# Queries of clusters without keys evened out by the mask alone, operand tiles by halves, and new engine orders, in a two-layer attention kernel

## The chip, the core and the metric

One NeuronCore of a Trainium2 chip runs the program. Its engines work side by side: TensorE (PE) multiplies matrices, PEld is its queue of weight loads, VectorE (DVE), ScalarE (ACT) and GpSimd (POOL) work elementwise, SyncE (SP) issues the DMA transfers. The metric is the device time of one run in microseconds. The kernel before took 713.66 us, the median of three runs (713.56 to 715.48).

## What is computed

The first layer is attention within clusters (4 batches, 8 heads, 768 positions, 64 wide, 16 clusters); its output is the input of a mixture of 4 attention experts, of which each position uses 2.

```python
def _attn_ref(q, k, v, centroids):
    ...
    q_assign = np.argmax(np.einsum('bhsd,hcd->bhsc', q_n, c_n), axis=-1)
    k_assign = np.argmax(np.einsum('bhsd,hcd->bhsc', k_n, c_n), axis=-1)
    mask = q_assign[:, :, :, None] == k_assign[:, :, None, :]
    scores = scale * np.matmul(q, k.transpose(0, 1, 3, 2))
    scores = np.where(mask, scores, -1000000000.0)
    ...  # softmax over keys, then attn @ v

def _moe_ref(x, w_gate, wq, wk, wv, wo):
    ...  # the two largest of x @ w_gate give the weights w
    for e in range(E):
        ...  # causal softmax attention with q, k, v = x @ wq[e], x @ wk[e], x @ wv[e]
        ye = a @ v @ wo[e]
        ...  # out += w * ye where e is one of the two
```

A query whose cluster holds no key has the same score, -1e9, for all keys: its attention is even over all 768 positions.

## The kernel before

The work is 24 steps: 16 *pairs* (two heads of one batch) and 8 expert pairs. Each has an operand part (`attention_operands`, `moe_operands`) and a core (`core`), and three sets of operand tiles `tk`, `tq` rotate, so that operands are made while earlier cores run. All products are in fp32r; a factor is split into a high part (rounded) and a low part (the rest), and high x high, high x low and low x high are added.

*Operands of a pair.* k and q are loaded and transposed (L626), copied from PSUM, and split; the low part is a subtraction on VectorE that reads PSUM (L639 for k, L782 for q). Scores with the centroids (L650), transposed (L662), give one-hot rows of the cluster by five VectorE steps (L668 to L676). Then keys are counted: six matmuls with ones (L685) and four VectorE steps that multiply the one-hot of q by min(count, 1) (L695), which clears the rows of queries without keys. The one-hot is transposed (L703), ScalarE makes `rows` (L706: 0 or 1 for q, 0 or -2^33 for k), and one matmul per head (L766) spreads over 64 rows whether a query has keys: the gate, with which VectorE multiplies q (L776; for the first half of pair 0 also L770, straight into `tq`). Only then q is split. SP moves the parts and the one-hot rows into `tk` and `tq`.

*Core of a pair.* Row scores (L1088: contraction over 64 high rows and 16 one-hot rows) give, by a maximum on VectorE (L1098, joined in L1104), the largest score of each query. The six columns of maxima are transposed (L1110; for pair 0 L1113), negated (L1126 or ScalarE) and moved into a row of `tq`. Scores (two matmuls, L1165 over 128 rows and L1166 over 97) then come out with mask and maximum in them, ScalarE takes exp (L1171), and p is weighted with v in a tile 64 columns wide (av, L1209). GpSimd and VectorE add up p (L478, L479), and matmuls of a tile 32 wide sum it over keys (L1233).

*Order.* Every engine's order is a written list of operation numbers, `ORDER`. A planner with prices for operations decides only how the five lists interleave and which buffer each tile takes. While it sees TensorE wait, and until the `av` buffer is first taken, it puts filler matmuls into TensorE's list (L1337: 256 columns of ones).

Of the kernel before, what the change touches and what calls it, by code (L numbers as in the profile page):

```python
# [244 lines left out]
class Plan:  # L245
# [1146 lines left out]
```

## Time and profile before

| | |
|---|---|
| median of 3 runs | 713.66 us (713.56 to 715.48) |
| profiled execution, span | 713.4 us |
| TensorE busy | 696.5 us (98%), 4562 matmuls |
| VectorE busy | 568.3 us (80%) |
| ScalarE busy | 363.0 us (51%) |
| GpSimd busy | 295.1 us (41%) |
| chain that ended last | 80% TensorE, 6% VectorE, 5% DMA |

The pairs run first, the expert pairs behind them. A matmul that the profile gives 0.34 us can start 0.17 us after the one before: successive matmuls overlap, so the spacing of the starts is what one costs.

### The profile page before, as it was taken

To read this page: it belongs to the slowest core of one execution; us is meant where nothing else is said; L and a number is where in the kernel's file an instruction comes from. 1 tells how busy PE (TensorE), PEld (TensorE's weight loads), DVE (VectorE), ACT (ScalarE), POOL (GpSimd) and SP (SyncE) were. 2 spreads that over 40 slices of the span, in tenths; PEclk is the share of its full clock that TensorE was granted. 3 is DMA by queue.
4 is the path that set the end of the run, shared out by engine and by line. 5 is a ranking of instruction groups with operands and counts; after the bars stand their busy time and mean duration, and the time that the engine had idled before them with its cause. 6 is when DMAs were issued, how large, how long until landed. Compare 5 with 4: busy or idle time off the path is not lost.

```text
span 713.4 us, 13574 instructions
## 1 busy us (share of the span) xinstructions
PE 696.5 (98%) x4562; PEld 521.5 (73%) x4562; DVE 568.3 (80%) x1293; ACT 363.0 (51%) x899; POOL 295.1 (41%) x236
## 2 busy tenths in 40 slices
PE   6999999999999999999999999999999999999997
PEld 4666768667677676676676678868977987987776
DVE  6979899878989888888888876895688688577843
ACT  4365657456466466456465633364345435333542
POOL 5033456564555574856778422241111203210410
PEclk9999999999999999999999999999999999999999
DMA  6695765677677576667586564455355555445223
GB/s 194 167 218 124 186 161 133 146 198 198 182 206 187 142 198 150 174 166 190 156 195 177 135 182 135 111 143 133 106 145 142 141 142 157 104 101 162 77 82 120
DMA packets 79793, 109.97 MB, mean 154 GB/s; under 512 B 23936, under 2 KB 63212, under 8 KB 79724
## 3 DMA queue, kind: packets, MB, share of 16 engines
q1 hardware_dynamic: 79724, 109.11, 58.3%
q8 instruction: 36, 0.59, 0.4%
q14 instruction: 33, 0.27, 0.1%
HBM read 36.54 MB, written 12.91 MB: 69 GB/s over the span
## 4 chain that ended last, share of the span: by engine, by line
PE 80%; DVE 6%; DMA 5%; SPq 4%; ACT 3%; issue 1%; ACTq 0%; DVEq 0%
PE av L1209 19%; PE st L1165 11%; PE row L1088 11%; PE st L1166 10%; PE misc L870 9%; PE misc L922 5%; SPq L466 4%; PE misc L1322 4%; PE misc L1233 3%; PE misc L626 2%; DMA tq<-hi 2%; DVE mx L1098 2%; DMA kt<-in_k_dram 2%; PE misc L650 1%; DMA vm<-x 1%
## 5 line engine op out<-in xcount | busy, mean ns | idle before, releaser
L1098 DVE TENSOR_REDUCE mx<-row 128x1 f32<-128x384 f32 (+1 forms) x442 | 232.6, 548 | 41.8 <-PE row L1088 37.8
L1165 PE MATMUL st<-tq,tk 128*128 128x384 f32 (+2 forms) x528 | 182.6, 348 | 3.2 <-ACT p L1171 2.1
L1171 ACT ACTIVATE p<-st 128x384 f32<-128x384 f32 (+2 forms) x304 | 130.0, 458 | 109.6 <-PE st L1166 68.2
L1166 PE MATMUL st<-tq,tk 97*128 97x384 f32 (+2 forms) x528 | 173.7, 332 | 0.0
L1088 PE MATMUL row<-tk,tq 80*128 80x384 f32 (+4 forms) x506 | 168.0, 359 | 1.7 <-DMA tq<-hi 1.2
L1165 PEld LDWEIGHTS st<-tq,tk 128*128 128x128 f32 x528 | 99.9, 189 | 21.4 <-issue 7.0
L1088 PEld LDWEIGHTS row<-tk,tq 80*128 80x128 f32 (+1 forms) x506 | 93.2, 189 | 27.3 <-DVE mx L1098 12.5
L1166 PEld LDWEIGHTS st<-tq,tk 97*128 97x128 f32 x528 | 100.3, 190 | 0.8
L478 POOL TENSOR_TENSOR acc<-acc,p 128x768 f32<-128x768 f32 (+2 forms) x34 | 58.6, 1723 | 85.8 <-DVE acc L479 52.7
L1176 POOL TENSOR_SCALAR_AFFINE_SELECT p<-p 128x256 f32<-128x256 f32 x48 | 20.5, 434 | 136.8 <-ACT p L1171 124.4
L1171 ACT ACTIVATE xl<-st 128x384 f32<-128x384 f32 x112 | 51.7, 492 | 31.5 <-PE st L1166 30.7
L1171 ACT ACTIVATE xh<-st 128x384 f32<-128x384 f32 x112 | 51.1, 497 | 28.0 <-PE st L1166 27.3
L473 ACT ACTIVATE hi<-misc 128x384 fp32r<-128x384 f32 x71 | 34.7, 493 | 54.6 <-PE misc L870 34.3
L1209 PE MATMUL av<-p,vt 128*64 128x384 f32 x320 | 60.0, 494 | 0.9 <-ACT p L1171 0.6
L478 POOL TENSOR_TENSOR acc<-acc,xh 128x768 f32<-128x768 f32 x28 | 51.4, 1839 | 21.9 <-DVE acc L479 8.1
L478 POOL TENSOR_TENSOR acc<-acc,xl 128x768 f32<-128x768 f32 x27 | 49.5, 1833 | 18.0 <-DVE acc L479 9.3
L479 DVE TENSOR_TENSOR acc<-acc,p 128x768 f32<-128x768 f32 (+2 forms) x57 | 46.8, 821 | 3.1 <-POOL acc L478 1.7
L1284 POOL TENSOR_TENSOR xt<-avu,rb 128x384 f32<-128x384 f32 x24 | 24.2, 1016 | 45.3 <-DMA rb<-rd 38.5
L1209 PE MATMUL av<-p,vm 128*64 128x384 f32 (+2 forms) x288 | 41.5, 423 | 0.0
L1209 PEld LDWEIGHTS av<-p,vt 128*64 128x64 f32 x320 | 21.0, 136 | 26.8 <-issue 23.9
L1209 PE MATMUL av<-xl,vt 128*64 128x384 f32 x224 | 40.2, 491 | 0.0
L1209 PE MATMUL av<-xh,vt 128*64 128x384 f32 x224 | 39.9, 490 | 0.0
(262 smaller groups left out, 1268.5 us busy)
## 6 DMA issues: line engine op xcount, KB each, us to landing
tq<-hi SPq DMA_DIRECT2D x91, 192.0 KB
tk<-hi SPq DMA_DIRECT2D x60, 192.0 KB
tk<-lo SPq DMA_DIRECT2D x46, 192.0 KB
tq<-lo SPq DMA_DIRECT2D x46, 192.0 KB
rb<-rd SPq DMA_DIRECT2D x46, 192.0 KB
vt<-in_v_dram SPq DMA_DIRECT2D x16, 384.0 KB
x<-xt SPq DMA_DIRECT2D x16, 384.0 KB
tk<-hi SPq DMA_DIRECT2D x16, 384.0 KB
```

What stands on the lines that cost most here:

```text
L466: SP.dma_start(*[x.bitcast(FT) if x.dtype == FR else x for x in (dst, src)])
L473: return op("act", t_act(n, sbuf), lambda: ACT.activation(dst(), src(), AF.Copy), due, after, use, alt=(MO["m_copy"], "dve", t_dve(n), lam ...
L478: ways = [("pool", t_pool(n), lambda: POOL.tensor_tensor(dst(), a(), b(), op=fn)), ("dve", t_dve(n), lambda: DVE.tensor_tensor(dst(), a(), ...
L479: ("dve", t_dve(n), lambda: DVE.tensor_tensor(dst(), a(), b(), op=fn))]
L870: PE.matmul(m()[:, :HW], w_[:, dc, es], x_[dc]()[:, c], start=(i == 0), stop=(i == 3 * DC - 1))
L922: PE.matmul(m()[:, :NV], x_[dc]()[:, ts], w_[:, dc, :], start=(i == 0), stop=(i == 3 * DC - 1))
L1088: PE.matmul(ps()[:, :w], Q[0:R, h, 0, c * 128:(c + 1) * 128], K[0:R, h, 0, i * w:(i + 1) * w], start=True, stop=True)
L1098: DVE.tensor_reduce(to, ps()[:, :w], axis=AX.X, op=OP.max)
L1165: PE.matmul(p()[:, o_:HW], K[:, h, 1, ks], Q[:, h, 1, qs], start=True, stop=False)
L1166: PE.matmul(p()[:, o_:HW], K[0:R, h, 0, ks], Q[0:R, h, 0, qs], start=False, stop=True)
L1171: ACT.activation(pt()[:, h, o_:HW], p()[:, o_:HW], AF.Exp, scale=SC)
L1209: PE.matmul(av()[h * 64:(h + 1) * 64, o_:HW], d["vv"](h, kc), pt()[:, h, o_:HW], start=(kc == 0), stop=(kc == nk - 1), tile_position=(0, 6 ...
```

## The change

The mask becomes -2^60 instead of -2^33, large enough that a score added to it vanishes: all scores of a query without keys are then equal, as in the reference, and counts, gate and its products go (L685, L695, L766, L770, L776, and the tile `blk`). q is split at once, from its copy in SBUF, and so is k; the low parts may be made by GpSimd or VectorE. The operand tiles hold both heads of a half side by side (`by_half`), so one transfer moves both; the first slot has high x high, one-hot rows and half of the low part of k (rows 96 to 127), the second high x low, the other half (rows 64 to 95) and the maximum (row 96). There are still two matmuls per score tile, over 128 and 97 rows. The maxima are transposed by an fp32r matmul with `identr` instead of an fp32 transpose. All five orders are new, and the planner's prices change (for filler and interleaving). The list of TensorE has 1433 operations instead of 1481, VectorE's 915 instead of 1004, GpSimd's 252 instead of 215. Filler goes from 98 matmuls to 7.

```diff
-BIG = float(2 ** 33)
+BIG = float(2 ** 60)
...
 ORDER = dict(
     pe="""
-8 4 15 0 13 1 185 18 189 194 20 196 199 361 23 25 37 42 201 52 50 54 68 66 58 204 64 206 70 60 62 56 78 72 219 82 80
...
+6 4 9 11 1 18 182 187 20 180 346 348 185 23 194 196 49 53 51 67 63 65 45 55 59 61 57 353 199 47 75 83 351 70 77 0 81
...
-    SWITCH = {(128, 64): 0.14, (128, 32): 0.14, (64, 128): 0.2, (32, 128): 0.2, (64, 32): 0.12, (32, 64): 0.12}
+    SWITCH = {(128, 64): 0.09, (128, 32): 0.09, (64, 128): 0.25, (32, 128): 0.225, (64, 32): 0.15, (32, 64): 0.12}
...
-        TK.append(consts.tile([128, 2, 2, S], FR, name=f"tk{s}"))
-        TQ.append(consts.tile([128, 2, 2, S], FR, name=f"tq{s}"))
-    MT = consts.tile([128, 2, 2, 128], FT)
-    M6 = consts.tile([128, 2, 2, HC], FT)
+        TK.append(consts.tile([128, 2, 2 * S], FR, name=f"tk{s}"))
+        TQ.append(consts.tile([128, 2, 2 * S], FR, name=f"tq{s}"))
+    MT = sb.tile([128, 2, 2, 128], FT, name="xt_1")
+    M6 = consts.tile([128, 2, 2, HC], FR)
+    identr = consts.tile([128, 128], FR)
+    DVE.tensor_copy(identr, identf)
...
-        for h in range(2):
-            POOL.memset(TK[s][64:128, h, 0, :].bitcast(FT), 1.0)
-            POOL.memset(TQ[s][64:128, h, 0, :].bitcast(FT), 0.0)
+        for T in (TK[s], TQ[s]):
+            POOL.memset(T[64:96, 0].bitcast(FT), 0.0)
+        POOL.memset(TK[s][96:128, 1].bitcast(FT), 1.0)
+
+    def by_half(T):
+        return T.rearrange("p s (t h j) -> p s t h j", t=2, h=2)
+
+    def by_head(T):
+        return T.rearrange("p s (h j) -> p s h j", h=2)
...
-                if name == "k":
...
+
+        def split(name, due):
+            hi, lo = x[name + "p"] = [work(tag, (128, 2, HW), FR) for tag in ("hi", "lo")]
+            his[name], los[name] = [], []
+            for h in range(2):
+                def part(t, h=h):
+                    return lambda: t()[:, h]
+                o = copy_op(part(hi), part(x[name]), HW, due, [xs[name][h]], [x[name], hi], True)
+                his[name].append(o)
+                los[name].append(sum_op(part(lo), part(x[name]), part(hi), HW, due + 0.5, [o], [x[name], hi, lo],
+                                        OP.subtract, "dve"))
+            return hi, lo
+        khi, klo = split("k", c1 + 1)
...
-        m3 = misc()
-
...
-                    PE.matmul(m3()[:, :32], onesb, ov[:, c, 2 + par],
-                              start=(c == 0 and par == 0), stop=(c == HC - 1 and par == 1))
-        o = op("pe", 0.2, go, c2 + 3, [o], [oh, m3])
...
-                    DVE.scalar_tensor_tensor(w, cnt[:, None, h].to_broadcast([128, HC, NK]), 1.0, w,
-                                             op0=OP.min, op1=OP.mult)
-        o = op("dve", 0.48, go, c2 + 4, [o], [oh, m3])
...
+        def put(T, rs, slots, src, due, after, d0=0, pars=(0, 1)):
+            nd = rs.stop - rs.start
+
             def go():
                 for par in pars:
-                    r, c = parts(par)
-                    dma(T[dst_rows, :, slot, c], src()[r])
-            return op("sp", len(pars) * [(0.69, 0.93)], go, due, after + free, use)
+                    x_ = src()[par * D + d0:par * D + d0 + nd].rearrange("d h j -> d (h j)")
+                    to = T[rs, slots, par].rearrange("d h j -> d (h j)") if slots != 2 else \
+                        T[rs, :, par].rearrange("d s h j -> d s (h j)")
+                    dma(to, x_ if slots != 2 else x_[:, None, :].to_broadcast([nd, 2, S]))
+            return op("sp", len(pars) * [(0.69, (1.86 if slots == 2 else 0.93) * nd / D)], go, due, after + free, [src])
...
-            def go(m=m, h=h):
-                PE.matmul(m()[:, :HW], blk[:, h], rows(), start=True, stop=True)
-            o = op("pe", t_mm(HW), go, due, [o_r], [m, rows])
...
-            def go(m=m, h=h):
-                DVE.tensor_tensor(m()[:, :HW], x["q"]()[:, h], m()[:, :HW], op=OP.mult)
-            o = op("dve", t_dve(HW), go, due + 0.5 + (3 if n == 0 else 0), [o], [m, x["q"]])
-            o = copy_op(lambda h=h, hi=hi: hi()[:, h], lambda m=m: m()[:, :HW], HW, due + 1, [o], [m, hi])
-            q_hi.append(o)
-
-            def go(m=m, h=h, hi=hi, lo=lo):
-                DVE.tensor_tensor(lo()[:, h], m()[:, :HW], hi()[:, h], op=OP.subtract)
-            q_lo.append(op("dve", t_dve(HW), go, due + 1.5, [o], [m, hi, lo]))
...
+        qhi, qlo = split("q", c2 + 9)
         if n:
-            need_row.append(put(low, Q, 0, hi, c2 + 15, q_hi, [hi]))
+            need_row += [put(K, low, 2, khi, c2 + 0.5, his["k"]), put(Q, low, 0, qhi, c2 + 0.5, his["q"])]
+            half_row, need_st = [], []
         else:
-            need_row2.append(put(low, Q, 0, hi, c2 + 15, q_hi, [hi], (1,)))
-        need_st += [put(high, Q, 1, hi, c2 + 16, q_hi, [hi]), put(low, Q, 1, lo, c2 + 16.5, q_lo, [lo])]
+            puts = [put(T, low, 0, src, c2 + 0.5, his[nm], 0, (par,))
+                    for par in range(2) for T, src, nm in ((K, khi, "k"), (Q, qhi, "q"))]
+            half_row = need_row[:2] + puts[:2]
+            need_row += puts[:3]
+            need_row2.append(puts[3])
+            need_st = [put(K, low, 1, khi, c2 + 0.6, his["k"])]
+        need_st.append(put(Q, low, 1, qlo, c2 + 0.7, los["q"]))
+        for slot, rs, d0 in ((0, slice(96, 128), 0), (1, slice(64, 96), 32)):
+            need_st += [put(K, rs, slot, klo, c2 + 0.8, los["k"], d0), put(Q, rs, slot, qhi, c2 + 0.9, his["q"], d0)]
...
+        def cols(T, rs, slot, h, half, c0, c1):
+            return by_head(T)[rs, slot, h, half * HW + c0:half * HW + c1] if moe else by_half(T)[rs, slot, half, h, c0:c1]
...
-                    PE.transpose(m()[:2 * HC, :128], M6[:, hf].rearrange("p h c -> p (h c)"), identf)
+                    PE.matmul(m()[:2 * HC, :128], M6[:, hf].rearrange("p h c -> p (h c)"), identr, start=True, stop=True)
...
-                        ks, qs = slice(kc * 128, (kc + 1) * 128), slice(hf * HW + o_, (hf + 1) * HW)
-                        R = MR + 1
-                        PE.matmul(p()[:, o_:HW], K[:, h, 1, ks], Q[:, h, 1, qs], start=True, stop=False)
-                        PE.matmul(p()[:, o_:HW], K[0:R, h, 0, ks], Q[0:R, h, 0, qs], start=False, stop=True)
-                    s_ = op("pe", 2 * t_mm(w), go, due + 0.1 * h, d["need_st"] + m_ops[hf], [p])
+                        kh, k0 = kc // HC, kc % HC * 128
+                        for i, (slot, rs) in enumerate(((1 - top, slice(0, 128)), (top, slice(0, MR + 1)))):
+                            PE.matmul(p()[:, o_:HW], cols(K, rs, slot, h, kh, k0, k0 + 128), cols(Q, rs, slot, h, hf, o_, HW),
+                                      start=(i == 0), stop=(i == 1))
```

**TensorE, middle of a pair**, behind the weighted sum of the pair before (av): counts, scores and row scores, the one-hot's transpose, and later (last row) the gate. Before:

```order
L1209 MATMUL av_1833<-xl_0_1767,vt_1057 64x384 x2
L685 LDWEIGHTS onesb
L685 MATMUL misc_1865<-oh_1859,onesb 128x32
...
L1165 MATMUL st_1874<-tq_104,tk_103 128x384
L1166 MATMUL st_1874<-tq_104,tk_103 128x384
L1088 MATMUL row_1882<-tk_105,tq_106 128x384
...
L703 LDWEIGHTS oh_1859
L703 MATMUL misc_1894<-identb,oh_1859 128x128
...
L1088 MATMUL row_1934<-tk_105,tq_106 128x384
L766 MATMUL misc_1936<-rows_1904,blk 128x384
```

Now, on TensorE at a like place:

```order
L1173 MATMUL av_1694<-xl_0_1595,vt_1533 64x384 x2
L684 LDWEIGHTS oh_1724
L684 MATMUL misc_1731<-identb,oh_1724 128x128
...
L1049 MATMUL row_1739<-tk_97,tq_98 128x384
L1129 MATMUL st_1741<-tq_96,tk_95 128x384 x2
L1049 MATMUL row_1747<-tk_97,tq_98 128x384
L1129 MATMUL st_1749<-tq_98,tk_97 128x384 x2
```

The transpose of the one-hot stands where the counts stood, and no gate follows.

**VectorE in the start**, from the one-hot of pair 0 (`oh`) to its first maxima (`mx`); `misc_321` and `misc_277` are the centroid scores of pair 1. Before:

```order
L676 TENSOR_TENSOR oh_266<-st_230,sm_239 128x384
L695 SCALAR_TENSOR_TENSOR oh_266<-misc_278,oh_266 128x3x16 x4
L730 COPY tk_103<-rows_301 16x384 x2
L770 TENSOR_TENSOR tq_104<-xq_185,st_319 64x384
L770 TENSOR_TENSOR tq_104<-xq_185,st_317 64x384
L776 TENSOR_TENSOR st_319<-xq_185,st_319 128x384
L776 TENSOR_TENSOR st_317<-xq_185,st_317 128x384
L668 TENSOR_REDUCE sm_348<-misc_321 128x24
L669 TENSOR_TENSOR misc_321<-misc_321,sm_348 128x384
L670 TENSOR_TENSOR misc_321<-misc_321,ramp 128x384
L1098 TENSOR_REDUCE mx_355<-row_346 128x1
L782 TENSOR_TENSOR lo_359<-st_319,hi_344 128x384
```

Now, on VectorE:

```order
L676 TENSOR_TENSOR oh_241<-st_208,sm_219 128x384
L476 CAST hi_264<-xq_174 128x384
L476 CAST xl_0_248<-xh_0_206 128x384
L710 COPY tk_95<-rows_257 16x384 x2
L668 TENSOR_REDUCE sm_284<-misc_277 128x24
L669 TENSOR_TENSOR misc_277<-misc_277,sm_284 128x384
L670 TENSOR_TENSOR misc_277<-misc_277,ramp 128x384
L675 TENSOR_REDUCE sm_284<-misc_277 128x24
L676 TENSOR_TENSOR oh_296<-misc_277,sm_284 128x384
L1060 TENSOR_REDUCE mx_308<-row_298 128x1
L1060 TENSOR_REDUCE mx_308<-st_310 128x1
```

Count steps and gate products are gone, two casts of high parts stand there, and the twelve maxima follow one another with nothing between.

**TensorE in the start**, at the first row scores of pair 0. Before (nine fillers stand ahead of these rows and 23 behind them):

```order
L662 MATMUL misc_321<-identf,s_274 128x128 x3
L1337 LDWEIGHTS onesb
L1337 MATMUL av_182<-onesb 128x256
...
L1088 MATMUL st_339<-tk_103,tq_104 128x384
L1088 MATMUL row_342<-tk_103,tq_104 128x384
L1088 MATMUL row_346<-tk_103,tq_104 128x384
```

Now, on TensorE:

```order
L662 MATMUL misc_277<-identf,s_269 128x128 x3
L1049 MATMUL row_298<-tk_95,tq_96 128x384
L1049 MATMUL row_300<-tk_95,tq_96 128x384
L1049 MATMUL st_302<-tk_95,tq_96 128x384
L1049 MATMUL st_306<-tk_95,tq_96 128x384
L1049 MATMUL st_310<-tk_95,tq_96 128x384
```

No filler stands around the first row scores; the seven that are left come behind the fifteenth of them and later.

## Rows read from the trace of the kernel before

**Rows 1.** The page: span, and the line of busy times.

```profile
span 713.4 us, 13574 instructions
...
PE 696.5 (98%) x4562; PEld 521.5 (73%) x4562; DVE 568.3 (80%) x1293; ACT 363.0 (51%) x899; POOL 295.1 (41%) x236
```

**Rows 2.** Busy us by stretch: length, PE, PEld, DVE, ACT, POOL, granted clock.

```profile
20.00:30.00 10.00, 9.48 (x68) 6.42 (x66) 9.90 (x25) 1.49 (x4) 0.00 (x0) 1.00 0.62 153
60.00:400.00 340.00, 336.02 (x2217) 236.88 (x2216) 291.01 (x633) 195.94 (x475) 207.69 (x130) 1.00 0.67 172
```

**Rows 3.** TensorE's groups: shapes, count, busy us, mean ns, idle before.

```profile
L1337 PE MATMUL av<-onesb 128*128 128x256 bf16 x98 | 14.6, 275 | 0.0
...
L766 PE MATMUL misc<-rows,blk 128*128 128x384 f32 x30 | 10.1, 348 | 0.0
...
L685 PE MATMUL misc<-oh,onesb 128*128 128x32 bf16 x96 | 5.1, 178 | 0.2
```

**Rows 4.** Timeline of TensorE in the pairs: start, us, line, shapes, count.

```profile
47.90 0.32 PE L685 MATMUL misc<-oh,onesb 128*128 128x32 bf16 x6
48.07 0.42 PE L1165 MATMUL st<-tq,tk 128*128 128x384 f32 x1
48.33 0.34 PE L1166 MATMUL st<-tq,tk 97*128 97x384 f32 x1
...
215.58 0.34 PE L766 MATMUL misc<-rows,blk 128*128 128x384 f32 x1
215.75 0.34 PE L1165 MATMUL st<-tq,tk 128*128 128x384 f32 x1
...
217.52 0.34 PE L1088 MATMUL row<-tk,tq 80*128 80x384 f32 x1
217.78 1.51 PE L1209 MATMUL av<-p,vt 128*64 128x384 f32 x8
...
222.27 0.27 PE L1110 MATMUL misc<-identf,M 128*6 128x128 f32 x1
222.30 0.42 PE L1165 MATMUL st<-tq,tk 128*128 128x384 f32 x1
222.56 0.34 PE L1166 MATMUL st<-tq,tk 97*128 97x384 f32 x1
```

**Rows 5.** Timeline of TensorE in the start.

```profile
4.71 1.51 PE L626 MATMUL misc<-identf,kt 128*128 128x128 f32 x6 [4.71 <-DMA kt<-in_k_dram]
...
11.38 0.49 PE L662 MATMUL st<-identf,s 128*128 128x128 f32 x3
...
34.25 0.42 PE L1165 MATMUL st<-tq,tk 128*128 128x384 f32 x1
```

**Rows 6.** Timeline of VectorE in the start; in brackets idle time before.

```profile
15.26 0.55 DVE L695 SCALAR_TENSOR_TENSOR oh<-misc,oh 128x48 bf16<-128x48 f32 x4 [0.41 <-PE misc L685]
17.02 0.74 DVE L730 CAST tk<-rows 16x384 fp32r<-16x384 f32 x2 [1.21 <-ACT rows L706]
...
18.73 1.01 DVE L776 TENSOR_TENSOR st<-xq,st 128x384 f32<-128x384 f32 x2
...
31.18 0.16 DVE L1104 TENSOR_REDUCE MT<-mx 128x6 f32<-128x12 f32 x1
```

**Rows 7.** VectorE's groups: low parts of k and count steps.

```profile
L639 DVE TENSOR_TENSOR lo<-misc,hi 128x384 fp32r<-128x384 f32 x30 | 16.4, 552 | 1.9 <-ACT xk L473 0.9 <-ACT hi L473 0.8 <-ACT p L1171 0.2
...
L695 DVE SCALAR_TENSOR_TENSOR oh<-misc,oh 128x48 bf16<-128x48 f32 x64 | 8.8, 200 | 5.0 <-PE misc L685 5.0
```

**Rows 8.** GpSimd's groups: an addition of 768 columns, a product of 384.

```profile
L478 POOL TENSOR_TENSOR acc<-acc,xh 128x768 f32<-128x768 f32 x28 | 51.4, 1839 | 21.9 <-DVE acc L479 8.1 <-DVE r L1261 5.2 <-ACT xh L1171 3.8
...
L1284 POOL TENSOR_TENSOR xt<-avu,rb 128x384 f32<-128x384 f32 x24 | 24.2, 1016 | 45.3 <-DMA rb<-rd 38.5 <-issue 6.7
```

**Rows 9.** The waits: engine, line, waited for; us, times, longest.

```profile
PEld row L1088 <- DVE mx L1098: 12.5, 29, 0.6
```

More of the change, by code (lines that the diff above doesn't have):

```diff
@@ L411, in t_mm, with t_tr @@
 def t_mm(n):
-    return max(n / 2400 + 0.015, 0.111)
+    return n / 2400 + 0.016
+def t_tr(n):
+    return n * 0.11
 def t_av(n):
-    return n / 600
+    return n / 597
 @with_exitstack
@@ L649, in go @@
                 h, nm = g // 2, "qk"[g % 2]
-                PE.matmul(m1()[32 * g:32 * g + 32, :HW], cbd[:, h0 + h].rearrange("p a c -> p (a c)"),
+                PE.matmul(m1()[32 * g:32 * g + 32, :HW], cbd[:, 2 * pr + h].rearrange("p a c -> p (a c)"),
                           x[nm]()[:, h], start=True, stop=True, tile_position=(0, 32 * g))
@@ L703, in go @@
                 PE.transpose(m4()[:, c * 128:(c + 1) * 128], oh()[:, c], identb)
-        o = op("pe", 0.25, go, c2 + 6, [o], [oh, m4, rows])
+        o = op("pe", 0.16, go, c2 + 6, [o], [oh, m4, rows])
         o_r = op("act", t_act(HW) + 0.18, lambda: ACT.activation(
@@ L710, in attention_operands @@
             op("act", 1.4, lambda: ACT.activation(nr[:, 1:2], nr[:, 0:1], AF.Exp, scale=0.0), c2 + 7, [o_r])
+        free = sets_free(n)
+        if n < 3:
+            free = [op("pool", 4.2, lambda: clear_rows(n % 3), t0 - 60)]
         def place_rows(T, i, pars=(0, 1)):
@@ L716, in go @@
                         r0 = h * 64 + i * 32 + par * NK
-                        dma(T[64:64 + NK, h, 0, par * HW:(par + 1) * HW], rows()[r0:r0 + NK])
-            return go
-        free = sets_free(n)
-        if n < 3:
-            free = [op("pool", 2.7, lambda: clear_rows(n % 3), t0 - 60)]
+                        dma(T[64:64 + NK, 0, par, h], rows()[r0:r0 + NK])
+            return op("sp", 2 * len(pars) * [(0.64, 0.25)], go, c2 + 8, [o_r] + free, [rows])
         if n:
-            need_row = [op("sp", 4 * [(0.64, 0.25)], place_rows(Q, 0), c2 + 8, [o_r] + free, [rows]),
-                        op("sp", 4 * [(0.64, 0.25)], place_rows(K, 1), c2 + 8.2, [o_r] + free, [rows])]
+            need_row = [place_rows(Q, 0), place_rows(K, 1)]
             need_row2 = []
@@ L736, in attention_operands @@
                         op("act", 2 * t_act(HW, True), go_q, c2 + 6.7, [o_r] + free, [rows]),
-                        op("sp", 2 * [(0.63, 0.25)], place_rows(K, 1, (1,)), c2 + 7, [o_r] + free, [rows])]
-            need_row2 = [op("sp", 2 * [(0.63, 0.25)], place_rows(Q, 0, (1,)), c2 + 15, [o_r] + free, [rows])]
-        def parts(par):
-            return slice(par * D, (par + 1) * D), slice(par * HW, (par + 1) * HW)
-        def put(dst_rows, T, slot, src, due, after, use, pars=(0, 1)):
+                        place_rows(K, 1, (1,))]
@@ L754, in attention_operands @@
-        half_row.append(put(low, K, 0, hi, c2 + 0.5, k_hi, [hi], (0,)))
-        need_row += [half_row[2], put(low, K, 0, hi, c2 + 0.5, k_hi, [hi], (1,))]
-        need_st = [put(low, K, 1, hi, c2 + 0.6, k_hi, [hi]), put(high, K, 1, lo, c2 + 0.7, k_lo, [lo])]
-        hi, lo = work("hi", (128, 2, HW), FR), work("lo", (128, 2, HW), FR)
-        q_hi, q_lo = [], []
-        for h in range(2):
-            m = misc() if n else plan.buf(psum, "st", (128, 512), FT, 3)
-            due = c2 + 8.5 + 2 * h
-            def go(m=m, h=h):
-                PE.matmul(m()[:, :HW], blk[:, h], rows(), start=True, stop=True)
-            o = op("pe", t_mm(HW), go, due, [o_r], [m, rows])
-            if n == 0:
-                def go(m=m, h=h):
-                    DVE.tensor_tensor(Q[0:D, h, 0, :HW], x["q"]()[0:D, h], m()[0:D, :HW], op=OP.mult)
-                o = op("dve", t_dve(HW), go, due + 0.2, [o] + free, [m, x["q"]])
-                need_row.append(o)
-                half_row.append(o)
-            def go(m=m, h=h):
-                DVE.tensor_tensor(m()[:, :HW], x["q"]()[:, h], m()[:, :HW], op=OP.mult)
-            o = op("dve", t_dve(HW), go, due + 0.5 + (3 if n == 0 else 0), [o], [m, x["q"]])
-            o = copy_op(lambda h=h, hi=hi: hi()[:, h], lambda m=m: m()[:, :HW], HW, due + 1, [o], [m, hi])
-            q_hi.append(o)
-            def go(m=m, h=h, hi=hi, lo=lo):
-                DVE.tensor_tensor(lo()[:, h], m()[:, :HW], hi()[:, h], op=OP.subtract)
-            q_lo.append(op("dve", t_dve(HW), go, due + 1.5, [o], [m, hi, lo]))
@@ L852, in go @@
             def go():
-                for h in range(2):
-                    POOL.memset(Q[64:96, h, 0, :].bitcast(FT), 0.0)
-            free = [op("pool", 1.35, go, t0 - 46, free)]
+                POOL.memset(Q[64:96, 0].bitcast(FT), 0.0)
+                POOL.memset(K[96:128, 0].bitcast(FT), 1.0)
+            free = [op("pool", 2.8, go, t0 - 46, free)]
         es = slice(ep * 128, (ep + 1) * 128)
@@ L887, in go @@
                     if slots == 2:
-                        dma(T[rows, h], r[:, None, :].to_broadcast([D, 2, S]))
+                        dma(T[rows, :, h], r[:, None, :].to_broadcast([D, 2, S]))
                     else:
-                        dma(T[rows, h, slots], r)
+                        dma(T[rows, slots, h], r)
             return op("sp", 2 * [(0.74, 2.05) if slots == 2 else (0.63, 0.93)], go, due, after + free, use)
@@ L1062, in core @@
         DUE = MO if moe else AT
+        top = 0 if moe else 1
         t_r = t0 + DUE["row"]
@@ L1085, in core, with go @@
                 used = [ps, mx] if nb == 2 else [ps]
-                def go(i=i, h=h, c=c, w=w, R=R, ps=ps):
-                    PE.matmul(ps()[:, :w], Q[0:R, h, 0, c * 128:(c + 1) * 128], K[0:R, h, 0, i * w:(i + 1) * w],
+                def go(hf=hf, i=i, h=h, cc=cc, w=w, R=R, ps=ps):
+                    PE.matmul(ps()[:, :w], cols(Q, slice(0, R), 0, h, hf, cc * 128, (cc + 1) * 128),
+                              by_head(K)[0:R, 0, h, i * w:(i + 1) * w] if moe else by_half(K)[0:R, 0, i, h],
                               start=True, stop=True)
@@ L1129, in go @@
                 def go(hf=hf, mr=mr):
-                    for h in range(2):
-                        dma(Q[MR:MR + 1, h, 0, hf * HW:(hf + 1) * HW], mr()[h * HC:(h + 1) * HC])
-                outs.append(op("sp", 2 * [(0.78, 0.05)], go, due + 0.5, [o] + sets_free(n), [mr]))
+                    if moe:
+                        for h in range(2):
+                            dma(cols(Q, slice(MR, MR + 1), top, h, hf, 0, HW), mr()[h * HC:(h + 1) * HC])
+                    else:
+                        dma(by_half(Q)[MR:MR + 1, top, hf].rearrange("r h j -> r (h j)"), mr())
+                outs.append(op("sp", (2 if moe else 1) * [(0.78, 0.05)], go, due + 0.5, [o] + sets_free(n), [mr]))
             else:
@@ L1234, in go @@
                               start=True, stop=True, tile_position=(0, 32 * g))
-            o = op("pe", t_av(QW), go, due + DUE["sums"], acc_ops, [m, acc, ssb], mode=32)
+            o = op("pe", t_av(QW) + 0.035, go, due + DUE["sums"], acc_ops, [m, acc, ssb], mode=32)
             def go_a(hf=hf, m=m):
```

58 lines of the change are left out of this document (16 added, 42 removed), and 327 rows, old and new, of tables (act, dve, pe, pool).

## The prediction

> **What bounds the kernel now.** I read the page first: TensorE is busy 696.5 of 713.4 us, 98% [rows 1]. The span is the profiled execution's own time; the median of the three timed runs, 713.66 us, is 0.3 us above it, so the sum below goes against 713.4 and is given as it stands. The stretches come next [rows 2]: from 60 to 400 us (attention) TensorE has 336.0 of 340 us, VectorE 291.0 and GpSimd 207.7. One stretch is different: from 20 to 30 us VectorE has 9.90 of 10 us, and TensorE's 9.48 there are no evidence, because much of it is filler: line 1337 issues 98 matmuls on a constant, 14.6 us, only where the planner saw TensorE wait [rows 3]. So there are two regimes: a start of 34 us that hangs on VectorE, where the first real score matmul begins at 34.25 us [rows 5], and the rest, where every TensorE instruction that goes away shortens the run, unless a wait takes its place.
>
> A busy sum by group misleads here, since matmuls overlap. I take the price of one from start to next start in the timeline [rows 4]: 0.17 to 0.18 us for any fp32r matmul of 384 columns.
>
> **The change, part by part, in us of the end time.**
>
> *Counts (line 685).* Six matmuls per pair go. From the first (47.90) to the next score matmul (48.07) they take 0.17, and that score matmul keeps its place for 0.26 (48.07 to 48.33) where its neighbour needs 0.18: a load of weights behind a very short matmul is not hidden. So 0.25 per pair. Of 16 pairs two lie in the start, under filler: 14 x 0.25 = **-3.5**. Bounds: -2.4 (only the 0.17) to -4.0 (all 16).
>
> *Gate on q (line 766).* Two matmuls per pair, 0.17 each (215.58 to 215.75): 28 outside the start, **-4.9**; bounds -4.7 to -5.6.
>
> *Transposed maxima (line 1110).* 46 fp32 transposes become fp32r matmuls with a constant. Now one costs 0.11: 0.03 to the next start (222.27 to 222.30), and 0.26 instead of 0.18 for the matmul there (to 222.56) [rows 4]. The new form isn't in the trace. Below: the gate matmul streams 384 columns in 0.175, so 128 would take 0.06 and save 0.05 each, 2.3 in all; more than the whole 46 x 0.11 = 5 can't go. Above: nothing gained, as the exposed load behind it stays. I take **-2.0**, near the gate row, the nearest; range -5 to 0.
>
> *Order of TensorE.* Same scores, row scores and weighted sums. Three kinds use the array in another tile size (av 64 wide; sums and centroid scores 32), and each entry costs: 217.52 to 217.78 is 0.26 instead of 0.175 [rows 4], so 0.09. In the order, two such groups stand back to back in 41 places before and in 24 now, which makes 206 changes of tile size 227. At about 0.1 each: **+2.1**; bounds 0 (leaving is free, fewer merges matter less) to +3.5 (0.15 a change plus rounding).
>
> *Start.* VectorE's chain to the first transposed maxima ends at 31.18, and the first scores follow 3.1 later [rows 5, 6]. Its one-hot was done at 14.85 (15.26 less the 0.41 it waited for the counts). Between them lay the count steps of two pairs (0.55 each, plus waits), four products with the first pair's gate and one with the next pair's (two take 1.01, so they are 0.46 apart), and three low parts. Now it is two casts (0.46 each), the K copy (0.74), the next pair's assignment (five steps of 384 columns at 0.58, 2.9), twelve maxima (0.46 each, 5.6) and the last small one: 10.3, plus about 1 of waits for the rows' transfer and for the next pair's centroid scores. The one-hot itself can come some 0.8 earlier, as the PSUM tile of k is free after one copy and no longer waits for its low part. So 14.0 + 11.3 = 25.3, first scores at 28.4, 5.8 earlier; 0.4 of that is two row matmuls that now come later. Gain 5.4 if TensorE runs at its full level, 2 if not (the second rival); I take **-4.0**.
>
> *VectorE's relief.* It loses 64 count steps (8.8 us), 34 gate products and, by the order, 45 of 64 low parts for attention that GpSimd takes over (552 ns each, 25) [rows 7]; it gains 15 full additions. Weight loads of row scores wait 29 times for VectorE's maxima, 12.5 us [rows 9]. About 8% of VectorE's work goes, but the worst waits sit where rows crowd, so I take **-2.0**; bounds -10 and +4 (a new order can put rows closer).
>
> *Operand transfers.* Q's high part no longer waits for one-hot, counts and gate, and each move writes both heads in one piece. As many bytes move as before, and the transfers lie beside TensorE's work on the pair before; covered, 0. If that cover were gone, it would be the slower rival's price.
>
> *GpSimd and ScalarE.* GpSimd adds 45 low parts of about 1 us (nearest: 1.02 for 384 columns, half of 1.84 for 768 [rows 8]) and drops 15 additions of 1.84: +17 us beside the 207.7 of attention [rows 2], off the path as long as they land before the scores want them. ScalarE's list stays the same length; its copies of k's high part read SBUF instead of PSUM. 0.
>
> Sum: 713.4 - 3.5 - 4.9 - 2.0 + 2.1 - 4.0 - 2.0 = **699.1**.
>
> **Rivals.**
>
> *More relief (693).* If the shorter chain to Q and the lighter VectorE take half of what is left of the 12.5 us [rows 9] and the start gives its full 5.4, some 6 more go. For it: row scores and maxima alternate one by one in both orders. Against it: between 60 and 400 us TensorE's own idle is only 4 us [rows 2].
>
> *The clock falls in the start (703).* Filler drops from 98 matmuls to 7, all of them just before the first scores. The granted clock reads 1.00, the 2.4 GHz level, in all stretches shown [rows 2], but the first six transposes take 1.51 us and three at 11.38 take 0.49, that is 0.21 against 0.11 apart [rows 5]: TensorE began at half pace, at 4.71, after doing nothing. Without filler, between the one-hot and the first rows it does little, and then one 0.18 us row per 0.46 us maximum. If it falls to 1.2 GHz, rows still hide under VectorE, but the transposes in the chain take double (0.5 to 1 us in all) and the first few us of scores run at half pace, 2 to 3 us. Then the start gains about 0: 703. The Trainium skill ("TensorE: Matmul & The Clock Gate", Part 1) says that the half rate is the default and that activity releases it, so by that rule the dropped filler costs the clock; the trace agrees on the first transposes, and shows nothing on a TensorE that is partly busy.
>
> *Late low parts, slower (719).* Place: GpSimd's queue in attention, where the low parts stand behind additions of 1.84 us. Scores need all parts, and SP issues transfers in order, so a late low part holds the next pair's one-hot rows and negative maxima behind it. Price: the delay beyond the slack, once per pair. At 1.35 us on 15 pairs that is 20 us, against the -14: 719. It decides from 1.1 us per pair on. For it: two additions ahead are 3.7 us. Against it: GpSimd is busy 207.7 of 340 us there [rows 2], and the added work raises that by only 5 points.
>
> *It doesn't carry through (713).* What TensorE no longer does turns into waits elsewhere, since the orders of all five engines are new. For it: VectorE is at 86% in attention. Against it: exactly that engine is relieved most.
>
> **How the numbers follow.** Forecast 699: 0.50. More relief: 0.17. Clock: 0.18, still faster. No gain: 0.08, of which 0.06 ends within 0.3% (2.1 us, about what a measurement of this kernel can tell from no change) and 0.02 just below it. Slower: 0.07, 0.06 of it by more than 0.3%, 0.01 within. Faster: 0.50 + 0.17 + 0.18 + 0.02 = 0.87; within: 0.07; slower: 0.06. Range: the low ends of the terms (start 5.4, relief 7, counts and gate at their bounds) give 691.5 (-1.4, -5, and -1.2 from counts and gate), the upper side must take in the clock case with no relief at all, 703 + 2, and a little of the case without gain: 691 to 707.
>
> **What would show it.** No count and gate instructions; score matmuls 0.18 apart as now; first scores near 28 us; from a transposed maximum to the second start behind it 0.23 us instead of 0.29; the first scores after it 0.18 apart (clock kept) or 0.35 (fallen); row weight loads waiting for VectorE less than 12.5 us; GpSimd's low parts done before their transfers are wanted. I am wrong if the stretch from 60 to 400 us isn't shorter per pair by about 0.5 us, if TensorE shows waits on transfers at the first score of each pair, or if the start ends later than 31 us.

## The result, and the profile after

The changed kernel takes **704.97 us** (median of 4 runs, 703.33 to 707.52) against 714.57 for the kernel before beside it: a ratio of 0.9859, 95% interval 0.9827 to 0.9891. The forecast was 699, the range 691 to 707. A second set of runs, on the chip of the first experiments, gave 705.03, ratio 0.9856 (0.9818 to 0.9894). In every execution whose span is on record, the time is 1.7 to 1.8 us above it.

The page of the changed kernel, span and busy times:

```profile
span 702.7 us, 13074 instructions
PE 684.0 (97%) x4343; PEld 510.8 (73%) x4343; DVE 537.2 (76%) x1154; ACT 365.1 (52%) x901; POOL 327.1 (47%) x268
```

Against [rows 1] the span lost 10.7 us and VectorE 31 us of work (5.5%), while GpSimd gained 32. The stretches, columns as in [rows 2]:

```profile
10.00:20.00 10.00, 6.92 (x36) 4.91 (x37) 6.74 (x12) 7.17 (x15) 7.08 (x6) 0.87 0.75 182
20.00:30.00 10.00, 9.46 (x34) 7.05 (x33) 9.60 (x21) 4.04 (x10) 6.04 (x6) 0.50 0.84 199
60.00:400.00 340.00, 335.93 (x2139) 233.49 (x2141) 281.37 (x546) 203.40 (x487) 202.70 (x143) 1.00 0.68 176
```

TensorE is as full in attention (60 to 400 us) as before, and the counts below show that it got further in the same time. Of VectorE's 31 us only 9.6 lie in that stretch, and GpSimd has 5.0 us less there, not more. From 20 to 30 us the granted clock is 0.50, the 1.2 GHz level: the clock rival's event took place. TensorE in the start, next to [rows 5]: transposes ahead of the one-hot, then the last row scores, filler and the first scores:

```profile
11.22 0.85 PE L662 MATMUL st<-identf,s 128*128 128x128 f32 x3
...
28.55 0.67 PE L1049 MATMUL row<-tk,tq 80*128 80x384 f32 x1
29.02 1.29 PE L1301 MATMUL av<-onesb 128*128 128x256 bf16 x5
30.99 0.72 PE L1129 MATMUL st<-tq,tk 128*128 128x384 f32 x3
```

First scores at 30.99 instead of 34.25. VectorE and GpSimd earlier in the start; the copy `tk<-rows` is to be held against the 0.74 at 17.02 in [rows 6], and the last small reduction against 31.18:

```profile
15.30 0.35 DVE L476 CAST xl<-xh 128x384 fp32r<-128x384 f32 x1
16.48 1.97 DVE L710 CAST tk<-rows 16x384 fp32r<-16x384 f32 x2 [0.82 <-ACT rows L687]
18.48 0.56 DVE L668 TENSOR_REDUCE sm<-misc 128x24 f32<-128x384 f32 x1
...
27.14 0.17 DVE L1066 TENSOR_REDUCE xt<-mx 128x6 f32<-128x12 f32 x1
```

```profile
16.16 2.08 POOL L480 TENSOR_TENSOR lo<-xq,hi 128x384 fp32r<-128x384 f32 x2 [2.03 <-DMA tk<-lo]
```

The same two copies of K's cluster rows take 1.97 us while GpSimd's low parts run. A transposed maximum in the new form, to be held against 222.27 to 222.56 in [rows 4]:

```profile
64.25 0.23 PE L1072 MATMUL misc<-identr,M 128*6 128x128 f32 x1
64.31 0.56 PE L1129 MATMUL st<-tq,tk 128*128 128x384 f32 x2
64.71 0.34 PE L1049 MATMUL row<-tk,tq 80*128 80x384 f32 x1
```

And the row that [rows 9] shows at 12.5, 29 times (PEld is the queue of weight loads):

```profile
PEld row L1049 <- DVE mx L1060: 18.9, 39, 0.9
```

The wait for VectorE's maxima grew though VectorE has less to do. The forecast had that only as the far bound of the relief, +4 ("a new order can put rows closer").

To place gains I count: the first of TensorE's 1056 weighted-sum matmuls begins at 38.9 us before and 35.8 after, the 768th at 480.3 and 469.1, the last at 696.6 and 687.5. So about 3 us come from the start and nearly all of the rest from the attention pairs. (The two orders don't put exactly the same other work ahead of these matmuls, so the counts are good to about 2 us.)

### The profile page after: what moved, and what is told of

Read it like the earlier page. It is cut to its first block, busy times and chain, and to the rows that moved or that the text cites. A ratio compares the mean times of both kernels' runs of the same rounds, so it can differ in the third digit from the quotient of the medians.

```text
span 702.7 us, 13074 instructions
## 1 busy us (share of the span) xinstructions
PE 684.0 (97%) x4343; PEld 510.8 (73%) x4343; DVE 537.2 (76%) x1154; ACT 365.1 (52%) x901; POOL 327.1 (47%) x268
## 2 busy tenths in 40 slices
DMA packets 68192, 110.15 MB, mean 157 GB/s; under 512 B 24496, under 2 KB 39324, under 8 KB 68124
## 4 chain that ended last, share of the span: by engine, by line
PE 89%; DMA 4%; SPq 3%; DVE 2%; issue 1%; ACT 1%; POOL 0%; ACTq 0%; POOLq 0%; DVEq 0%
PE st L1129 25%; PE av L1173 22%; PE row L1049 14%; PE misc L827 10%; PE misc L879 5%; PE misc L1286 4%; PE misc L625 3%; SPq L468 3%; PE misc L1197 3%; DMA tq<-mr 2%; PE misc L653 1%; DVE mx L1060 1%; PE st L1286 1%; DMA kt<-in_k_dram 1%; DMA rb<-rd 1%
## 5 line engine op out<-in xcount | busy, mean ns | idle before, releaser
L1129 PE MATMUL st<-tq,tk 128*128 128x384 f32 (+5 forms) x1056 | 248.6, 339 | 3.2 <-DMA tq<-mr 2.0
L1129 PEld LDWEIGHTS st<-tq,tk 128*128 128x128 f32 (+1 forms) x1056 | 181.5, 190 | 20.7 <-issue 7.5
L1049 PE MATMUL row<-tk,tq 80*128 80x384 f32 (+3 forms) x506 | 172.2, 365 | 2.9 <-DMA tq<-hi 1.4
L1049 PEld LDWEIGHTS row<-tk,tq 80*128 80x128 f32 x506 | 93.6, 192 | 42.0 <-DVE mx L1060 18.9
L480 POOL TENSOR_TENSOR acc<-acc,p 128x768 f32<-128x768 f32 (+2 forms) x37 | 66.0, 1784 | 58.1 <-DVE acc L481 34.6
L1135 ACT ACTIVATE xh<-st 128x384 f32<-128x384 f32 x112 | 53.0, 493 | 34.6 <-PE st L1129 32.1
L480 POOL TENSOR_TENSOR acc<-acc,xh 128x768 f32<-128x768 f32 x24 | 44.1, 1838 | 23.8 <-DVE acc L481 22.0
L1058 DVE TENSOR_TENSOR row<-row,tri 128x128 f32<-128x128 f32 x96 | 28.2, 293 | 21.9 <-PE row L1049 21.4
L480 POOL TENSOR_TENSOR acc<-p,p 128x768 f32<-128x768 f32 (+1 forms) x14 | 23.4, 1674 | 40.9 <-ACT p L1135 40.6
L480 POOL TENSOR_TENSOR acc<-acc,xl 128x768 f32<-128x768 f32 x18 | 33.2, 1843 | 18.2 <-ACT xl L1135 13.2
L1248 POOL TENSOR_TENSOR xt<-avu,rb 128x384 f32<-128x384 f32 x29 | 29.7, 1035 | 17.9 <-DMA rb<-rd 11.3
L480 POOL TENSOR_TENSOR lo<-xk,hi 128x384 fp32r<-128x384 f32 x20 | 20.4, 1032 | 33.3 <-ACT hi L475 12.8
```

What stands on the lines that cost most here:

```text
L480: ways = [("pool", t_pool(n), lambda: POOL.tensor_tensor(dst(), a(), b(), op=fn)), ("dve", t_dve(n), lambda: DVE.tensor_tensor(dst(), a(), ...
L1049: PE.matmul(ps()[:, :w], cols(Q, slice(0, R), 0, h, hf, cc * 128, (cc + 1) * 128), by_head(K)[0:R, 0, h, i * w:(i + 1) * w] if moe else by ...
L1058: DVE.tensor_tensor(e, e, tri, op=OP.add)
L1129: PE.matmul(p()[:, o_:HW], cols(K, rs, slot, h, kh, k0, k0 + 128), cols(Q, rs, slot, h, hf, o_, HW), start=(i == 0), stop=(i == 1))
L1135: ACT.activation(pt()[:, h, o_:HW], p()[:, o_:HW], AF.Exp, scale=SC)
L1248: e.tensor_tensor(xt().rearrange("d (p c t) -> d t c p", c=HC, t=2)[:, par], avu()[:, c].rearrange("d (c p) -> d c p", c=HC), rb()[:, c].r ...
```

## Experiments

Each was timed against the kernel before on the same chip, and ratios are to that kernel. Three chips were used (the kernel before took 715.07, 715.57 and 716.53 us on them), and the changed kernel, 705.0 us or 0.986, was run again on the first alone. So ratios are what to compare, and the difference of two of them is good to some 3 us.

**The start.** Base and filler. The second kernel moves operation 0, which opens the filler, in TensorE's order:

```
-6 4 9 11 1 18 182 ... 351 70 77 0 81
+6 4 9 0 11 1 18 182 ... 351 70 77 81
```

> The changed kernel once more, as the base for the other runs on this chip: 705 us (703 to 707), 0.986 of the kernel before. Both theories on the start expect the same here: the granted clock at 0.5 from about 17 to 30 us, first scores at 31.0 us.

> The changed kernel with the operation that opens the filler put fourth in TensorE's order instead of just before the first scores, so that 70 filler matmuls instead of 7 run in the waits of the start. Theory A (the clock that fell costs time): the granted clock stays at 1.0 from 10 us on, the transposes of the one-hot chain take half, the first scores come at 29 to 30 us instead of 31.0 and run 0.18 apart at once: 702 to 703.5 us. Theory B (the start hangs on VectorE's chain alone, the clock costs nothing): 704.5 to 705.5 us, first scores at 30.5 to 31.2 us.

Base: 705.03, clock 0.50 from 20 to 30 us again, first scores at 30.79. With filler: 708.97 us, 12 runs, ratio 0.9909 (0.9879 to 0.9939). Its stretch and its VectorE rows:

```profile
20.00:30.00 10.00, 9.24 (x54) 6.33 (x55) 8.91 (x20) 4.27 (x11) 5.15 (x5) 1.00 0.82 202
```

```profile
14.92 0.35 DVE L476 CAST xl<-xh 128x384 fp32r<-128x384 f32 x1
15.31 0.74 DVE L710 CAST tk<-rows 16x384 fp32r<-16x384 f32 x2
16.87 0.56 DVE L668 TENSOR_REDUCE sm<-misc 128x24 f32<-128x384 f32 x1 [0.82 <-PE misc L662]
```

```profile
16.23 1.96 POOL L480 TENSOR_TENSOR lo<-xq,hi 128x384 fp32r<-128x384 f32 x2 [2.04 <-DMA tk<-lo]
```

The clock stays at 1.00 and the first scores come at 29.32, as theory A said of the trace. No time is gained: 708.97 is outside what either theory said. In the trace the 1.5 us are gone by the 768th weighted sum (470.9 against 469.1).

Nor does this run show that the clock gave the 1.5 us. A later run (the maxima in fp32, below) changes nothing in the start, has the seven filler matmuls of the changed kernel, and its clock falls, too; yet its first scores come at 29.43:

```profile
20.00:30.00 10.00, 9.21 (x38) 6.99 (x38) 9.21 (x21) 4.15 (x11) 5.20 (x5) 0.61 0.84 205
```

```profile
15.69 0.74 DVE L710 CAST tk<-rows 16x384 fp32r<-16x384 f32 x2 [0.38 <-ACT rows L687]
...
26.30 0.17 DVE L1066 TENSOR_REDUCE xt<-mx 128x6 f32<-128x12 f32 x1
```

```profile
29.43 0.87 PE L1129 MATMUL st<-tq,tk 128*128 128x384 f32 x4
```

With this start six traces have their first scores at 29.43 to 30.99, and the two with more filler at 29.32 and 29.89. What the low clock costs can be read behind VectorE's last small reduction: from there to the first scores 3.85 us pass in the changed kernel, where the clock reads 0.50 up to 30 us, and 3.13 here, where it is back at 1.00 from 28 us on. That is 0.7 us there.

The run with filler also bears on the copy: one us earlier, it ends at 16.05, before GpSimd's low parts begin at 16.23, and takes 0.74 again. But nothing is gained by it there: VectorE then waits 0.82 us for the next pair's centroid scores (16.87 above), and from the end of the one-hot to the last small reduction 12.3 us pass with the fast copy and 12.0 in the changed kernel with the slow one. The direct test of the copy did not come about:

```
-  los[name].append(sum_op(..., HW, due + 0.5, [o], ...
+  los[name].append(sum_op(..., HW, due + 0.5, [o] + first_copy, ...
```

> The changed kernel; the two low parts of the first pair's q on GpSimd wait until VectorE has copied K's cluster rows. Theory A (GpSimd's subtractions slow VectorE's copy beside them): the copy takes 0.74 us for its two instructions instead of 1.97, VectorE's chain to the first transposed maxima ends 1.0 to 1.2 us earlier, and the kernel takes 703.5 to 704.3 us. Theory B (the copy is slow for another reason, as its place right behind ScalarE's write): it stays at 1.9 to 2.0 us, 705 us.

> The two edits to the start together: filler from the fourth place on, and low parts of the first pair's q behind VectorE's copy of K's cluster rows. If both theories A hold and act on the same chain, their gains add: first scores at 28 to 29 us, 701 to 702.5 us. If only one of the two matters: 703 to 704 us; if neither: 705 us.

The first gave 704.8 us (0.984, 0.9793 to 0.9887), with the low parts at 15.81 and the copy, 1.91 long, behind them at 16.19. They did not wait: the dependence entered the plan only, and every engine runs the list of the changed kernel. The run tells nothing on its theories. The second is therefore the filler once more, with the same lists as there: 705.29 us, 0.9865 (0.9823 to 0.9907), copy 0.74. So two sets of runs of what the traces show as one program, on one chip, differ by 3.7 us, and neither beats the changed kernel.

**The transposed maxima.**

```
-  M6 = consts.tile([128, 2, 2, HC], FR)
+  M6 = consts.tile([128, 2, 2, HC], FT)
-  PE.matmul(m()[:2 * HC, :128], M6[:, hf]..., identr, start=True, stop=True)
+  PE.transpose(m()[:2 * HC, :128], M6[:, hf]..., identf)
```

> The changed kernel with the 46 maxima transposed as fp32 again, as in the kernel before. Theory A (what such a matmul costs is the weight load behind it, which a shorter matmul only exposes more): 704.5 to 705.5 us, no difference. Theory B (the fp32r form saved the 2 us of the prediction and something else took them): 706.5 to 707.5 us, and the second start behind a transposed maximum comes 0.05 us later.

707.64 us, 0.9877 (0.9833 to 0.9922): the median is near theory B's, but against 0.9856 (0.9818 to 0.9894) the times can't tell. The trace can. Over the 20 maxima that have two scores behind them, the median from maximum to second score is 286.5 ns in fp32 (29 + 258) and 288.5 in fp32r (62 + 227.5, the changed kernel's second trace), where two scores are 177 apart. In both forms the weight loads of the two scores begin 2 to 3 and 113 ns behind the start of the maximum, and the second load ends at 304 to 305, about when its score starts. So theory A: the loads set the time to the second score, and the form of the matmul in front of them doesn't.

**What TensorE no longer does.** Ahead of the transposes of the centroid scores, in 14 pairs:

```
+  for c in range(2 * HC):
+      PE.matmul(m2()[:, :32], onesb, onesb[:, :32], ...)
+  for h in range(2):
+      PE.matmul(m2()[:, :HW], identr, identr[:, None, :].to_broadcast([128, HC, 128]), ...)
```

> The changed kernel with TensorE's part of the counts and of the gate put back, without use: for 14 pairs six matmuls of 32 columns and two fp32r matmuls of 384 columns on constants, ahead of the transposes of the centroid scores; nothing waits for them and VectorE gets no more work. Theory A (what TensorE no longer issues is what the change gained behind the start): 14 x (0.25 + 0.35) = 8.4 us more, 712 to 714 us. Theory B (it was partly hidden in waits, and VectorE's relief is the gain): 705 to 709 us.

713.2 us, ratio 0.9959 (0.9929 to 0.999): 8.2 us more than the changed kernel by the medians, 7.4 by the ratios, for 8.4 expected. One pair in the trace:

```profile
207.19 0.32 PE L663 MATMUL misc<-onesb 128*128 128x32 bf16 x6
207.36 0.60 PE L665 MATMUL misc<-identr 128*128 128x384 f32 x2
207.79 0.49 PE L667 MATMUL misc<-identf,s 128*128 128x128 f32 x3
```

From 207.19 to 207.79 is 0.60 us, as priced. Theory A, within the 3 us that the ratios allow. (The trace is of the slowest of the 12 runs, 716.96 us.)

The other direction, the same removal on the old orders. VectorE's count steps and gate products go as well (for the first half of pair 0 a copy of q takes the product's place), and the larger mask constant is used. Tiles and transfers stay those of the kernel before:

```
-  PE.matmul(m3()[:, :32], onesb, ov[:, c, 2 + par], ...)
-  DVE.scalar_tensor_tensor(w, cnt[:, None, h]..., 1.0, w, op0=OP.min, op1=OP.mult)
-  PE.matmul(m()[:, :HW], blk[:, h], rows(), start=True, stop=True)
-  DVE.tensor_tensor(m()[:, :HW], x["q"]()[:, h], m()[:, :HW], op=OP.mult)
```

> The kernel before, with its own orders, tiles and filler (88 matmuls now), without counts and gate: the larger mask constant, q's high and low parts taken from q itself. Theory A (removal is the whole gain behind the start, and the new orders with their tile-size changes cost 1.7 us): 713.7 - 8.4 - 1 to 3 at the start = 702.5 to 704.5 us, not slower than the changed kernel. Theory B (the gain needs the new orders and the low parts on GpSimd): 706 to 711 us.

713.02 us, 0.9956 (0.9926 to 0.9986): theory A is refuted, and theory B's 706 to 711 is missed as well. The first weighted sum comes 2.3 us earlier than before, the 768th 3.3, the last 2.3: nearly the whole gain is the start, and 8.4 us of TensorE work behind it are gone for nothing. The waits, first the kernel before:

```profile
PE row L1088 <- DVE mx L1098: 0.3, 1, 0.3
```

```profile
PE row L1078 <- DVE mx L1088: 2.1, 3, 1.1
```

```profile
PEld row L1078 <- DVE mx L1088: 18.9, 38, 1.4
```

The waits of PE lie inside those of PEld in every trace, so they don't add up: from 12.5 to 18.9, 6.4 us more. But 18.9 is also what the changed kernel waits, and it is 8 us faster. The spacing of TensorE's starts says more: each matmul is charged with the time from the start before it to its own, in us between the first and the 768th weighted sum (single matmuls differ between the orders).

| | before | removal alone | changed kernel |
|---|---|---|---|
| all | 441.4 | 440.5 | 433.3 |
| counts and gate, with the waits ahead of them | 12.7 | 0 | 0 |
| row scores | 69.0 | 74.1 | 76.9 |
| scores | 145.0 | 149.5 | 144.0 |
| transposed maxima | 6.7 | 8.5 | 6.3 |
| all else | 208.0 | 208.4 | 206.1 |

What TensorE no longer did in the old orders, it waited, ahead of row scores and of scores in about equal parts. In the changed kernel row scores take still longer, and it is the scores that don't (76.0 and 145.7 in its second trace). Why they don't, no run shows.

So removal with the old orders gives 0.9956, everything else that is new with the work put back 0.9959, and both together 0.986. "Everything else" is more than orders: the operand tiles by halves, with their transfers in 68192 packets instead of 79793, are in it, and no run takes them apart from the orders.

**Which part of the new orders.** Low parts back on VectorE, then the other way round:

```
 pool:  -538 -687 -689 ...   (35 operations of L480, lo<-, behind 60 us)
 dve:   +538 +687 +689 ...   (each at its planned time)
```

> The changed kernel with 35 low parts of the attention pairs behind 60 us moved from GpSimd back to VectorE, each put into VectorE's order where it was planned on GpSimd: 35 x 0.55 = 19 us more on VectorE, 36 us less on GpSimd. Theory A (VectorE's load is not what TensorE waits for there): 704.5 to 706 us, the wait of the row scores' weight loads for the maxima within 3 us of 18.9. Theory B (the relief is real, and other things of the new orders took it): 707 to 712 us, with that wait above 24 us.

> The kernel before without counts and gate, as it took 713 us, with 42 low parts moved from VectorE to GpSimd, each at the time at which VectorE had it; all other orders as before. Theory A (relief of VectorE is what was missing): 704 to 708 us. Theory B (places decide: GpSimd takes 1.05 us where VectorE takes 0.55, stands behind additions of 1.84, and the transfers behind a late low part come late, the slower rival of the prediction): 714 us or more, with TensorE's waits on transfers above 5 us where the kernel before has 2.

Back on VectorE, in orders made for the other split: 721.23 us, 1.0061 (1.0028 to 1.0093), slower than the kernel before. Theory B, and by more than it said:

```profile
PE row L1048 <- DVE mx L1059: 11.7, 16, 1.6
```

```profile
PEld row L1048 <- DVE mx L1059: 34.6, 56, 1.9
```

```profile
160.00:180.00 20.00, 17.73 (x94) 13.35 (x94) 15.59 (x28) 9.48 (x22) 6.79 (x4) 0.83 0.68 173
```

The changed kernel in the same stretch:

```profile
160.00:180.00 20.00, 19.94 (x127) 13.57 (x123) 15.67 (x33) 10.38 (x25) 11.32 (x8) 1.00 0.77 187
```

Where the waits crowd, the granted clock falls as well (0.83 there and 0.91 from 380 to 400 us). After two waits of 1.2 and 1.7 us before 171.1, the clock reads 0.50 from 172 to 176 us, and from 171.6 to 177.4 the 18 matmuls start 0.32 us apart instead of 0.18: some 2.5 of the 16 us are the clock's.

But on the old orders relief does nothing: 42 low parts on GpSimd and 717.08 us, 1.0007 (0.9975 to 1.0039), 4 us slower than without the move.

```profile
60.00:400.00 340.00, 331.10 (x2097) 228.74 (x2096) 267.63 (x514) 193.28 (x470) 243.70 (x166) 0.99 0.66 170
```

VectorE has 267.63 us instead of 282.56 in the run without the move, and TensorE is less busy. TensorE's waits on transfers behind 30 us are 4.3 us, where the run without the move has 2.0: less than theory B's 5, but not nothing. So theory B's price is right, and its mechanism is neither shown nor excluded.

Last, all five orders refitted by moving single operations against the planner's own model (here the head of TensorE's, with the low parts on VectorE):

```
-6 4 9 11 1 18 182 187 20 180 346 348 185 23 194 196 49 53 51 67 63 65 45 55 ...
+6 4 9 11 1 18 182 187 20 180 346 348 185 23 194 196 55 49 65 63 47 67 53 51 61 0 ...
```

> The kernel with 35 low parts on VectorE that took 721 us, with the same instructions on the same engines; only the orders of the five engines are refitted to it, by moving single operations. Theory A (VectorE's load decides): it has the same 19 us more on VectorE as that kernel, so it stays slow, 716 to 722 us. Theory B (the places of the low parts between row scores and maxima decide, the load does not): 702 to 708 us, like the changed kernel, and the waits of row scores for maxima fall from 46 us to below 25.

> The kernel before without counts and gate that took 713 us (its tiles, its low parts on VectorE, its split of work between the engines), with the orders of the five engines refitted by moving single operations; fillers fall to some 20. Theory A (the gain needs the low parts on GpSimd): 711 to 715 us as without the moves. Theory B (the gain needs new places, since the old orders turned the removed TensorE work into waits for the maxima): 703 to 709 us, with these waits below the 21 us of that run.

> The changed kernel with its orders refitted by moving single operations, and 68 operations of GpSimd and 13 copies moved between engines on the way (GpSimd has 184 instead of 252 operations, VectorE 970 instead of 915). If places decide and there is still room in them: 701 to 704 us, faster than the changed kernel's 705.0; if GpSimd's relief of VectorE is what carries the change: 708 us or more.

With low parts on VectorE and new places: 710.67 us, 0.9928 (0.9895 to 0.9962), between the two theories. Its instructions on VectorE are those of the 721 us run, and 10.6 us are gone:

```profile
PE row L1048 <- DVE mx L1059: 6.2, 6, 1.6
```

```profile
PEld row L1048 <- DVE mx L1059: 18.8, 29, 1.9
```

34.6 us of waits became 18.8. Places matter at the same load; whether the 5.6 us that are left are the load or the fit stays open. Removal with refitted orders: 720.86 us, 1.0085 (1.0054 to 1.0117), slower than either theory said, waits 24.6. The changed kernel refitted, with operations moved between engines: 714.86, 0.9996 (0.9969 to 1.0022), waits 21.5; that is the slow side of what was expected, but it mixes the new split with the new places. Both are slower than what they started from, so the model misses something of the chip; what, wasn't looked for. So no run shows that places alone, with the low parts left on VectorE, carry the change. No version tried is clearly faster than the changed kernel.

## Why the prediction was right, and where it was not

- **Counts and gate, -8.4: the size was right, the condition missing.** The work costs 8.2 us (7.4 by the ratios) in the new orders and next to nothing in the old ones. I called every TensorE instruction that goes away a gain "unless a wait takes its place"; in the old orders a wait does, and the rival *doesn't carry through* (713) is just what removal alone measures.
- **VectorE's relief, -2.0: the failed step.** I made it a term of its own, taken off the 12.5 us of [rows 9]. That wait did not shrink (18.9, and 16.2 in the second trace), and VectorE lost 5.5% of its work, not about 8%. The 8.4 arrive only where low parts on GpSimd and the rest of the new kernel come together: put back in the same orders, the low parts cost 16 us, with refitted orders 5.6 us are left; moved on old orders, they gain nothing. A condition was priced as a summand. Whether the orders or the new tiles and transfers make the other half of that condition stays open.
- **Transposed maxima, -2.0: 0.** The upper bound held. I took the gate matmul's streaming time as the nearest row, while the row at 222.27 pointed at the load behind, and the loads are what the traces show.
- **Tile sizes, +2.1: not measured by itself.** 8.2 for the work and 3 for the start are already 0.5 more than the 10.7 that the span lost, so what tile sizes and new waits cost together is small.
- **Start, -4.0: about -3, by other steps.** First scores at 30.99 instead of 28.4, and the 2.6 us can be placed. The one-hot was done at 15.1 instead of 14.0, no earlier than before (three transposes ahead of it, at 11.22, take 0.85 us at half pace, where [rows 5] has 0.49); from there to the last small reduction it took 12.0 us instead of 11.3; and from there to the first scores 3.85 instead of 3.1, which is the price of the low clock there. Among the steps of the middle part the copy beside GpSimd took 1.2 us more than its row of before, but no run shows that a faster copy brings the first scores forward. The Trainium skill ("SBUF — State Buffer", Who interferes with whom) says that VectorE in its two-port modes and GpSimd exclude each other for a whole instruction, whoever is first; the copy at 1.97 us beside GpSimd and 0.74 without it agrees, and in five traces each half of the slow copy ends 0.21 to 0.22 us behind the GpSimd subtraction that was under way when it began. I had counted GpSimd's new low parts as off the path and did not look at what they lie beside.
- **The rivals.** *Clock*: the event came, but of its price only 0.7 us shows before the first scores and some 0.4 in the transposes ahead of the one-hot. *More relief*: no. *Late low parts*: not in the changed kernel, where scores waited for transfers only 2.6 us in the pairs; and the 17 us more of GpSimd in attention did not come (202.70 against 207.69).

The profiled span is 702.7, 3.6 above the sum of 699.1: maxima 2, relief 2 and start 1 are missing, and the tile sizes cost less than the 2.1 that I added. The median, 705, is another 2.3 above that span: 1.8 is time outside the span, as in every execution, and 0.5 is the choice of execution. The prediction set the median, 713.66, beside a span of 713.4 and read the 0.3 between them as that difference; with the 1.7 of every other execution the profiled one took some 715.1 (an estimate), so it was a slower one, and the forecast lacked some 1.4 us from its first paragraph on.

That 705 lies in the range is in part luck. The largest term holds under a condition that the prediction had only among its rivals, and the upper end had been drawn for the clock case without relief; the relief did fail, but the room for the clock was filled by other misses.

## What to carry to other kernels

When two engines feed each other in turn, a TensorE that reads 98% busy does not make its instructions worth their time: test the removal alone, in the old order, before pricing it. A row of waits is no price either: two kernels here wait 18.9 us for the same maxima and are 8 us apart. Before calling an earlier step a gain of an edit, look how much that step moves in traces that the edit doesn't touch. Price the load behind a very short matmul, not its streaming. Look at what a step given to GpSimd will lie beside on VectorE.

## What the runs showed of the hardware that was not expected

- Two fp32 to fp32r copies of 16x384 on VectorE, SBUF to SBUF: 0.74 us alone, 1.91 to 2.20 beside GpSimd subtractions of 128x384, in five traces.
- A transposed maximum costs TensorE 0.11 us between scores in fp32 and in fp32r alike (287 and 288.5 ns to the second score, less 177); the second weight load behind it ends at 304 to 305 ns in both.
- In attention, the granted clock fell to 0.83 over 20 us with TensorE busy 17.73 of them, in a kernel that waits more; the changed kernel reads 1.00 there.
- In the start, six traces with the same filler have their first scores at 29.43 to 30.99; holding the granted clock at 1.00 with 70 filler matmuls gave 29.32 and no gain in time.
